# A gated state-space and mixture kernel on one core: input chunks in pairs of 512 columns, and x*D seeded into PSUM before the matmuls

## The chip, the cores and the metric

The kernel runs on one core of one Trainium2 chip. The metric is the device time of one execution in microseconds (us), the median over several runs. The time before was 252.28 us (251.54 to 252.75, three runs). The kernel's own *span* in a profile is 1.7 to 1.9 us shorter than the time in the same run; profile positions below are counted from the span's start. PE is TensorE (matmuls), PEld its weight loads, DVE is VectorE, ACT is ScalarE, POOL is GpSimd, SP is SyncE. PSUM is the memory that matmuls write and accumulate into. "PEclk" is the share of the full TensorE clock that was granted.

## The reference, cut to what matters

```python
x = A_x                                             # (1, 2048, 1024) bf16
g = sigmoid((x * gate_w).sum(-1, keepdims=True))    # one gate per token

# A: a state-space model with a diagonal recurrence over 2048 tokens
Bu = einsum("bld,pd->blp", x, B_bar)                # complex
h_t = Lam_bar * h_(t-1) + Bu_t
a = 2 * einsum("blp,dp->bld", h, C).real + x * Dskip

# B: a small expert for the 8 tokens with the largest r = x @ w_r
idx = argsort(-r)[:8];  xs = x[idx]
y = (silu(xs @ w_gate) * (xs @ w_up)) @ w_down      # 1024 -> 3584 -> 1024
b = x  with  sigmoid(r[idx]) * y  added at idx

out = g * a + (1 - g) * b
```

## The kernel before

Tokens are handled in eight chunks of 256, or sixteen row blocks of 128. *S1* computes V = B x for a chunk (1024 matmuls of 256 columns in all). VectorE turns V by sine and cosine tables, runs the recurrence as a scan, and turns back to H. *S2* computes C H for a row block (512 matmuls). ScalarE empties PSUM: V out of S1, and the gated output out of S2.

```python
def s1u(k, cp, c, pl):            # 8 matmuls, 256 columns wide
    ...
    for dc in range(KD):
        nc.tensor.matmul(vps[:, pl, c, :], lhsT=BT[pl][:, dc, ct * P:(ct + 1) * P],
                         rhs=xT[k][:, dc, :], start=(dc == 0), stop=(dc == KD - 1))

def s1e(k, cp):                   # ScalarE empties the bank pair
    nc.scalar.copy(out=V[k][:, :, 2 * cp:2 * cp + 2, :], in_=vp.pop((k, cp))[:])
...
def scale_x(b):                   # ScalarE: the factor g*D + (1-g) of a row block, f32
    es[b] = gpool.tile([P, D], F32, name="e32", tag="e32")
    nc.scalar.activation(out=es[b][:], in_=Dbc[:], func=ACT.Identity,
                         scale=gcol[:, b:b + 1], bias=omgcol[:, b:b + 1])

def mul_e(b):                     # VectorE: x * factor, an f32 operand; stored as the first part of the output
    xt = xts[b]
    nc.vector.tensor_tensor(out=xt[:], in0=xt[:], in1=es.pop(b)[:], op=ALU.mult)
    if b < NTT - 2:
        nc.gpsimd.dma_start(out2d[b * P:(b + 1) * P, :], xt[:])
...
def s2(b, dh):                    # 16 matmuls, 512 columns wide; the output is added in memory by fin(b)
    zps = ps_s2.tile([P, 512], F32, name="zps", tag="zps")
    for ct in range(NCT):
        for pl in range(2):
            nc.tensor.matmul(zps[:], lhsT=H[k][...], rhs=CT[pl][:, ct, dsl],
                             start=(ct == 0 and pl == 0), stop=(ct == NCT - 1 and pl == 1))
    nc.scalar.activation(out=ots[b][:, dsl], in_=zps[:], func=ACT.Copy, scale=gcol[:, b:b + 1])

def fin(b):
    nc.gpsimd.dma_start(out2d[b * P:(b + 1) * P, :], ots.pop(b)[:], accum_op=ALU.add)
```

The expert's weights (22 MB) stream through buffers that the chunks of x have left. `load_w` loads the next piece as soon as a buffer is free, and a buffer is free when the matmuls on its old piece are done. So between two bursts of expert matmuls lies a *refill window*, in which the pieces for the next burst have to arrive.

```python
def load_w():
    while nload[0] < NW and free_w:
        ...
        nc.sync.dma_start(...)           # wgu: 448 KB, wd: 512 KB a piece
def moe_item(i):
    w, pool, tag = wq.pop(i)
    ...                                  # matmuls on this piece
    free_w.append((pool, tag))
    load_w()
...
gu_pos = [(4, 3)] * 4 + ...              # where in the order each gate/up piece is used
d_pos = [(7, 4)] * 7 + [(8, 4)] * 7      # the down projection: two bursts of seven pieces
at((8, 4.15), fin_a)                     # then the update is finished and scattered
at((8, 4.17), lambda: (fin_b(), scatter_upd()))
```

A position (n, i) is a place in the order of TensorE's work: stage n, after its unit i.

## Time and profile before

| | before |
|---|---|
| time, median (range) | 252.28 us (251.54 to 252.75) |
| span of the profiled run | 251.0 us |
| PE busy | 243.4 us, 97% |
| DVE busy | 232.9 us, 93% |
| S1 matmuls | 1024 of 256 columns, 114.3 us |
| last product of VectorE that S2 needs | ends at 241.6 us |
| wait of PE for expert weights | none |

The page of the kernel before: busy time by engine; PE, granted clock and DMA in 40 slices of the span (a 9 is 90% or more); the chain of waits by engine and by line; and the costliest group of matmuls (busy us, mean ns of one, idle before).

```profile
PE 243.4 (97%) x1970; PEld 164.1 (65%) x1986; DVE 232.9 (93%) x230; ACT 101.3 (40%) x143; POOL 41.6 (17%) x58
...
PE   7799999999999999999999999999999999999994
...
PEclk9999999999999999999999999999999999999999
...
PE 77%; SPq 18%; DMA 2%; issue 1%; DVE 0%
...
L253 PE MATMUL vps<-xT,BT 128*128 128x256 bf16 x1024 | 114.3, 273 | 2.0 <-DMA BT<-in_A_B_re_dram 0.9
```

TensorE is busy from the first slice to the last, at full clock, and the chain of waits is mostly its own work. The mean of 273 ns is the latency of one matmul; what counts is the distance between two of them, read from a stretch in the timeline: 64 matmuls of 256 columns take 7.15 us there (112 ns each at the edges of a stretch, 109 in the middle).

### The profile page before, as it was taken

How to read it: one execution, taken by the hardware profiler on the slowest of the kernel's cores; microseconds unless marked ns; L12 is line 12 of the kernel's file. 1: busy time of each engine (PE TensorE's matmuls, PEld its weight loads, DVE VectorE, ACT ScalarE, POOL GpSimd, SP SyncE). 2: the span in 40 equal slices, each digit the busy share in tenths (PEclk: the TensorE clock that was granted, in tenths of full speed). 3: DMA queues.
4: the chain of work that ended last, by engine and by line, in shares of the span. 5: the costliest groups of instructions: out<-in, count | busy, mean ns of one | idle time of the engine just before them, and what ended most of it. 6: DMA issues, size and time to landing. Idle time of an engine off the chain costs nothing.

```text
span 251.0 us, 4661 instructions
## 1 busy us (share of the span) xinstructions
PE 243.4 (97%) x1970; PEld 164.1 (65%) x1986; DVE 232.9 (93%) x230; ACT 101.3 (40%) x143; POOL 41.6 (17%) x58
## 2 busy tenths in 40 slices
PE   7799999999999999999999999999999999999994
PEld 5588889884668547874477744886448864454453
DVE  1899999999999499999999999999999999999993
ACT  3679992525213321634221371221722335264411
POOL 4020000000000057301400140013100500141520
PEclk9999999999999999999999999999999999999999
DMA  7999999999920202809795588759998739957082
GB/s 167 212 184 221 190 218 246 232 216 278 278 93 3 73 0 86 170 9 346 149 357 181 206 224 280 248 215 335 269 309 273 187 68 292 301 134 198 3 167 84
DMA packets 63492, 48.31 MB, mean 192 GB/s; under 512 B 49504, under 2 KB 51168, under 8 KB 63472
## 3 DMA queue, kind: packets, MB, share of 16 engines
q1 hardware_dynamic: 59056, 37.23, 57.5%
q0 software_dynamic: 4224, 10.53, 17.4%
q8 instruction: 15, 0.25, 0.4%
q10 hardware_dynamic: 192, 0.27, 0.3%
q14 instruction: 5, 0.04, 0.1%
HBM read 27.55 MB, written 8.40 MB: 143 GB/s over the span
## 4 chain that ended last, share of the span: by engine, by line
PE 77%; SPq 18%; DMA 2%; issue 1%; DVE 0%
PE zps L716 41%; PE vps L253 28%; SPq L89 8%; SPq L98 8%; PE zl L730 3%; PE pgu L635 3%; DMA xT<-in_A_x_dram 2%; SPq L85 2%; PE y L647 1%; PE zc L468 1%; SPq L77 0%; DVE ot L735 0%; PE aT_ps L662 0%; PE xselT_ps L561 0%; PE zs_ps L577 0%
## 5 line engine op out<-in xcount | busy, mean ns | idle before, releaser
L253 PE MATMUL vps<-xT,BT 128*128 128x256 bf16 x1024 | 114.3, 273 | 2.0 <-DMA BT<-in_A_B_re_dram 0.9
L253 PEld LDWEIGHTS <-BT 128*128 128x128 bf16 x1024 | 99.4, 98 | 16.4 <-issue 2.3
L716 PE MATMUL zps<-CT,H 128*128 128x512 bf16 x465 | 104.0, 379 | 1.0 <-issue 0.3
L716 PEld LDWEIGHTS <-H 128*128 128x128 bf16 x480 | 46.2, 98 | 55.8 <-issue 1.9
L288 DVE TENSOR_TENSOR_SCAN U<-d,U 128x2048 bf16<-128x2048 f32 (+1 forms) x20 | 61.7, 3127 | 0.4
L258 ACT CAST V<-vps 128x1024 bf16<-128x1024 f32 x32 | 32.2, 1008 | 60.3 <-PE vps L253 60.3
L719 ACT ACTIVATE ot<-zps,gcol 128x512 bf16<-128x512 f32 x30 | 20.6, 687 | 67.9 <-PE zps L716 67.9
L693 POOL DMA_DIRECT2D out_dram<-xt x14 | 7.8, 559 | 93.2 <-DVE xt L691 92.6
L687 ACT ACTIVATE e<-Dbc,omgcol,gcol 128x1024 f32<-128x1024 bf16 x16 | 18.9, 1233 | 0.0
L691 DVE TENSOR_TENSOR xt<-xt,e 128x1024 bf16<-128x1024 bf16 x16 | 18.8, 1218 | 0.0
L278 DVE TENSOR_TENSOR V<-V,nTi 128x4096 bf16<-128x4096 bf16 (+1 forms) x10 | 16.5, 1652 | 0.5
L277 DVE TENSOR_TENSOR U<-V,T2tab 128x4096 bf16<-128x4096 bf16 (+1 forms) x10 | 16.5, 1646 | 0.5
L279 DVE TENSOR_TENSOR U<-U,V 128x4096 bf16<-128x4096 bf16 (+1 forms) x10 | 16.5, 1652 | 0.3
L554 POOL DMA_INDIRECT xsel<-in_A_x_dram,idx_c x1 | 6.4, 6383 | 61.6 <-ACT ot L719 61.6
L313 DVE TENSOR_TENSOR U<-U,S2tab 128x4096 bf16<-128x4096 bf16 (+1 forms) x8 | 16.2, 2025 | 0.3
L315 DVE TENSOR_TENSOR H<-H,U 128x4096 bf16<-128x4096 bf16 (+1 forms) x8 | 16.2, 2025 | 0.3
L311 DVE TENSOR_TENSOR H<-U,Ctab 128x4096 bf16<-128x4096 bf16 (+1 forms) x8 | 16.1, 2018 | 0.0
L740 POOL DMA_DIRECT2D out_dram<-ot x14 | 14.3, 1044 | 2.0 <-ACT ot L719 2.0
L682 POOL DMA_DIRECT2D xt<-in_A_x_dram x12 | 8.2, 680 | 13.6 <-DMA out_dram<-xt 13.6
L346 DVE TENSOR_TENSOR_SCAN U<-D,U 128x1024 bf16<-128x1024 f32 x4 | 8.9, 2278 | 0.0
L635 PE MATMUL pgu<-wgu,xsel 128*32 128x448 bf16 x128 | 7.4, 355 | 0.0
L730 PE MATMUL zl<-CT,H 128*128 128x256 bf16 (+1 forms) x47 | 7.1, 306 | 0.1
(145 smaller groups left out, 128.4 us busy)
## 6 DMA issues: line engine op xcount, KB each, us to landing
wgu<-in_B_w_gate_dram SPq DMA_DIRECT2D x16, 448.0 KB, 5.8
wgu<-in_B_w_up_dram SPq DMA_DIRECT2D x16, 448.0 KB, 5.9
wd<-in_B_w_down_dram SPq DMA_DIRECT2D x12, 512.0 KB, 6.4
out_dram<-xt POOLq DMA_DIRECT2D x14, 256.0 KB, 2.9
out_dram<-ot POOLq DMA_DIRECT2D x14, 256.0 KB, 5.7
xt<-in_A_x_dram POOLq DMA_DIRECT2D x12, 256.0 KB, 4.9
xt<-in_A_x_dram SPq DMA_DIRECT2D x4, 256.0 KB, 4.8
wd<-in_B_w_down_dram SPq DMA_DIRECT2D x4, 256.0 KB, 7.3
```

The source lines that it names most:

```text
L89: nc.sync.dma_start_transpose(BT[pl][:, :, c0 * P:c1 * P], Bsrc[pl][c0 * P:c1 * P, :])
L98: nc.sync.dma_start_transpose(CT[pl][:, :, d0_:d0_ + 512], Csrc[pl][d0_:d0_ + 512, :])
L253: nc.tensor.matmul(vps[:, pl, c, :], lhsT=BT[pl][:, dc, ct * P:(ct + 1) * P], rhs=xT[k][:, dc, :], start=(dc == 0), stop=(dc == KD - 1))
L258: nc.scalar.copy(out=V[k][:, :, 2 * cp:2 * cp + 2, :], in_=vp.pop((k, cp))[:])
L277: nc.vector.tensor_tensor(out=u, in0=v, in1=T2tab[:, :, c0:c1, :], op=ALU.mult)
L278: nc.vector.tensor_tensor(out=v, in0=v, in1=bc(nTi, c0, c1), op=ALU.mult)
L279: nc.vector.tensor_tensor(out=u, in0=u, in1=V[k][:, ::-1, c0:c1, :], op=ALU.add)
L288: nc.vector.tensor_tensor_scan(out=fl, data0=d0[:, c0:c1, :].rearrange("p c t -> p (c t)"), data1=fl, initial=0.0, op0=ALU.mult, op1=ALU.add)
L687: nc.scalar.activation(out=es[b][:], in_=Dbc[:], func=ACT.Identity, scale=gcol[:, b:b + 1], bias=omgcol[:, b:b + 1])
L691: nc.vector.tensor_tensor(out=xt[:], in0=xt[:], in1=es.pop(b)[:], op=ALU.mult)
L716: nc.tensor.matmul(zps[:], lhsT=H[k][:, pl, ct, tl * P:(tl + 1) * P], rhs=CT[pl][:, ct, dsl], start=(ct == 0 and pl == 0), stop=(ct == NCT ...
L719: nc.scalar.activation(out=ots[b][:, dsl], in_=zps[:], func=ACT.Copy, scale=gcol[:, b:b + 1])
```

## The change

Its intent is to give TensorE fewer and wider matmuls, and to take work from VectorE. Chunks of x lie in pairs, so that most of S1 runs with 512 columns. The gates of all tokens come from 32 wide matmuls instead of 128 narrow ones. From row block 4 on, VectorE computes x*D in bf16, ScalarE copies it into the PSUM bank of S2, and S2's matmuls add onto it; ScalarE scales x by 1 - g for the first part of the output. All of S1 now runs earlier, and the order at the end is S2 of chunks 4 to 7 back to back. The expert's weights come in slots of two pieces, in four big buffers.

```diff
-            nc.tensor.matmul(vps[:, pl, c, :], lhsT=BT[pl][...], rhs=xT[k][:, dc, :], ...)
+        o = vp[m, ct][:, pl, k0:k1, :].rearrange("p k t -> p (k t)")
+            nc.tensor.matmul(o, lhsT=BT[pl][...], rhs=X[m][:, dc, k0 * LC:k1 * LC], ...)
...
-    def gate_cols(k0, k1):
-                    nc.tensor.matmul(zc[:, j, :], lhsT=xT[k][:, dc, tl * P:(tl + 1) * P], rhs=rg[:, dc, :], ...)
+    def gate_rows():
+                nc.tensor.matmul(zr[32 * m:32 * m + 32, :], lhsT=rg[:, dc, :], rhs=X[m][:, dc, :], ...)
...
+    def skip_d(k):
+        for b in (2 * k, 2 * k + 1):
+            xd[b] = xdpool.tile([P, D], BF16, name="xd", tag="xd")
+            nc.vector.tensor_tensor(out=xd[b][:], in0=xts[b][:], in1=Dbc[:], op=ALU.mult)
+    def skip_x(*bs):
+        for b in bs:
+            nc.scalar.activation(out=xt[:], in_=xt[:], func=ACT.Copy, scale=omgcol[:, b:b + 1])
+            if b < NTT - 2:
+                nc.scalar.dma_start(out2d[b * P:(b + 1) * P, :], xt[:])
+    def preset(b, dh):
+            z = pool.tile([P, w], F32, name="zps", tag=tag)
+            nc.scalar.copy(out=z[:], in_=xd[b][:, d_:d_ + w])
...
-                nc.tensor.matmul(zps[:], ..., start=(ct == 0 and pl == 0), ...)
+                nc.tensor.matmul(zps[:], ..., start=(fresh and ct == 0 and pl == 0), ..., skip_group_check=not fresh)
...
-    d_pos = [(7, 4)] * 7 + [(8, 4)] * 7
+    pos = ... + [(7, 0.9)] * 2 + [(8, 1.9)] * 4 + [(9, 0.9)] * 3        # slots of two pieces
+        at(pos[s], lambda s=s: moe_slot(s))
-    at((8, 4.15), fin_a)
+    at((9, 0.92), fin_a)
```

The down projection now has a burst of four slots (eight pieces) and one of three (six pieces), and its second burst stands three S2 units behind the first, where before it stood four behind.

## The prediction

> **What bounds it now.** TensorE. The busy table gives PE 243.4 of 251.0 us (97%) at full clock; the chain of waits is almost all matmuls (L716 41%, L253 28%) after the transposing loads of the start. VectorE is nearly co-critical: 232.9 us; its timeline has one gap over 1 us between 12 and 246 us (3.1 us at 84 us), and its last scan product ends at 241.6 us, just before the final matmuls (240.6 to 247.7) need it. ScalarE has 40%.
>
> **Removed.**
> - S1 goes from 1024 matmuls of 256 columns to 480 of 512 plus 64 of 256. In the windows view an undisturbed S1 stretch takes 13.95 us for 128, 109 ns each; S2's 512-column ones take about 213. Only about 2.5 ns per removed matmul go: about 1.5 us, perhaps 3 us with the early ones (110 to 112 ns). The Trainium skill ("TensorE: Matmul & The Clock Gate", section "Wait — 56ns, not 53.3ns?") gives 2.5 ns fixed per warm matmul; the trace agrees.
> - Gate columns: 128 small matmuls (3.5 us) become 32 wide ones in four column groups plus four transposes, an estimate of 2.3 us from the 57 ns of the grouped MoE matmuls: 1.2 us less.
> - VectorE: twelve of sixteen f32-operand skip products (1.22 us) become bf16 products (0.68 us, as the bf16 add of that shape): 6.5 us less. Six gate operations go to ACT: 1 us.
>
> **Added.** ScalarE: 24 preset copies into PSUM and 12 row scalings replace twelve 1.23 us scalings; S1 drains are twice as many, half as wide; about 10 us more, hidden: presets are issued before the previous drain. The risk is correctness: the skill's "PSUM — Partial Sum Buffer", section "The four PSUM rules", says engine writes do not set the bits that make a matmul accumulate; the bank must have been written by matmuls before, and it has.
>
> **Moved.** All S1 now runs earlier, S2 of blocks 4 to 7 back to back at the end. Walking the new order by hand with trace durations:
> - VectorE waits about 1.4 us at the start, since V0 is complete only after six paired column tiles, and still ends its last product near 236 to 237 us, 4 to 5 us earlier than before.
> - PE's gate pass needs the last x chunk near 61 us, about 1 us after PE gets there.
> - The token gather now ends near 104 us (index near 95, plus 8 to 9 us as in the trace), while PE wants it for its transposes near 101.5: a PE wait of about 2 to 3 us that before did not exist (before: landed 98.6, used 107.3).
> - MoE weights come in pairs into four big slots; at the late bursts the refill windows (12 to 14 us for about 3 MB) leave little margin: 0 to 2 us.
>
> **On the critical path.** PE saves about 4 us, plus about 1 us of early waits, and gives back about 3 us in new waits. VectorE's 4 us become slack. Predicted: 249.4 us, range 246.0 to 252.8. Faster by over 2%: 0.17; within 2%: 0.77; slower: 0.06.
>
> **What would show it.** S1 at about 213 ns per 512-column matmul; PE busy near 239 us; skip products at 0.68 us and VectorE near 226 us; PE idle before the gate pass (about 1 us) and before the gathered-token transposes (2 to 3 us); no PE wait on presets; VectorE waiting in the final blocks or finishing over 2 us before the last matmuls.
>
> **What would make it wrong.** A gather faster than assumed (then near 247); PE waiting for weights longer; ScalarE late with drains or presets, because its own output-DMA issues wait in its queue; VectorE still gating the last blocks.

## More of the kernel before

The end of TensorE's timeline before: start us, length us, group, and in brackets any wait before it. The lines with `y<-wd,aT` are the two bursts of the down projection.

```profile
206.11 1.71 PE L647 MATMUL y<-wd,aT 128*32 128x256 bf16 x56
207.98 13.76 PE L716 MATMUL zps<-CT,H 128*128 128x512 bf16 x62 [0.16 <-issue]
221.67 1.71 PE L647 MATMUL y<-wd,aT 128*32 128x256 bf16 x56
223.31 17.44 PE L716 MATMUL zps<-CT,H 128*128 128x512 bf16 x78
240.59 7.11 PE L730 MATMUL zl<-CT,H 128*128 128x512 bf16 x47
```

The second burst starts at 221.67 with no bracket behind it, so it did not wait. The refill window is 221.67 - 206.11 = 15.6 us. How much of it the transfers needed is in the windows view of the same stretch (window, busy us of each engine, granted clock, share of the 16 DMA engines that was busy, GB/s):

```profile
216.00:218.00 2.00, 2.00 (x11) 0.93 (x10) 2.00 (x3) 0.00 (x0) 0.56 (x1) 1.00 1.04 320
218.00:220.00 2.00, 1.95 (x10) 0.88 (x10) 2.00 (x2) 0.69 (x1) 0.54 (x1) 1.00 1.07 402
220.00:222.00 2.00, 2.00 (x21) 0.91 (x22) 2.00 (x2) 0.22 (x1) 0.00 (x0) 1.00 0.39 156
```

The DMA engines are full until 220 us and fall quiet before 222. The last load of these weights was issued at 210.6 us and took 11.6 us to land, so it landed at 222.2, 16.1 us after the first burst began; the matmuls on its piece, the seventh, started at 223.0.

## The result, and the profile after

| | before | after |
|---|---|---|
| time, median (range), 4 runs each | 252.51 us (251.54 to 252.93) | 255.94 us (255.70 to 256.63) |
| ratio | | 1.0146, 95% interval 1.0108 to 1.0183 |
| span of the profiled run | 251.0 us | 254.8 us |
| PE busy | 243.4 us | 245.1 us |
| DVE busy | 232.9 us | 227.1 us |
| wait of PE for expert weights | 0 | 3.8 us |
| mean granted clock | 0.999 (profiled run) | 0.984 to 0.993 |

A ratio is the mean time of one kernel's fast runs over that of the other's from the same rounds, so it is not quite the ratio of the medians. The changed kernel is correct, and 1.5% slower.

The page of the kernel after, the same parts:

```profile
PE 245.1 (96%) x1414; PEld 115.7 (45%) x1414; DVE 227.1 (89%) x231; ACT 117.5 (46%) x203; POOL 33.5 (13%) x50
...
PE   7899999999999999999999999999999999589995
...
PEclk9999999999999999999999999999999999959999
...
PE 85%; DMA 9%; SPq 4%; issue 0%; DVE 0%
...
L771 PE MATMUL zps<-CT,H 128*128 128x512 bf16 x480 | 108.1, 386 | 0.0
L266 PE MATMUL vps<-X,BT 128*128 128x512 bf16 x480 | 105.3, 379 | 0.2 <-DMA BT<-in_A_B_im_dram 0.2
L282 PE MATMUL vps<-X,BT 128*128 128x256 bf16 x64 | 7.3, 273 | 1.2 <-DMA BT<-in_A_B_re_dram 0.8
```

Most of it went as intended: S1 costs 105.3 + 7.3 = 112.6 us instead of 114.3, VectorE lost 5.8 us of work. But slice 35 of PE has a 5, and the granted clock has a 5 one slice later. The end of TensorE's timeline after:

```profile
206.48 1.93 PE L672 MATMUL y<-wd,aT 128*32 128x256 bf16 x64
208.34 10.53 PE L771 MATMUL zps<-CT,H 128*128 128x512 bf16 x48
218.81 1.06 PE L672 MATMUL y<-wd,aT 128*32 128x256 bf16 x32
221.61 0.40 PE L672 MATMUL y<-wd,aT 128*32 128x256 bf16 x8 [1.74 <-DMA wd<-in_B_w_down_dram]
224.11 0.62 PE L672 MATMUL y<-wd,aT 128*32 128x256 bf16 x8 [2.09 <-DMA wd<-in_B_w_down_dram]
224.66 20.07 PE L771 MATMUL zps<-CT,H 128*128 128x512 bf16 x80
244.56 7.11 PE L787 MATMUL zps<-CT,H 128*128 128x512 bf16 x48
```

The second burst now starts 218.81 - 206.48 = 12.3 us after the first. The last two pieces are not there: TensorE waits 1.74 and 2.09 us. And then 80 matmuls take 20.07 us. At the pace of the stretch between the bursts (48 in 10.53 us, with the latency of the last counted in) they would take about 17.4. The windows view of the same stretch, same columns, says why:

```profile
218.00:220.00 2.00, 1.87 (x37) 1.05 (x35) 1.97 (x4) 0.69 (x1) 0.00 (x0) 1.00 1.06 401
220.00:222.00 2.00, 0.39 (x8) 0.20 (x8) 1.97 (x3) 0.00 (x0) 0.00 (x0) 1.00 1.11 291
222.00:224.00 2.00, 0.01 (x3) 0.00 (x0) 1.97 (x3) 0.00 (x0) 0.00 (x0) 0.80 0.13 27
224.00:226.00 2.00, 1.89 (x12) 0.65 (x12) 1.97 (x3) 1.20 (x4) 0.00 (x0) 0.50 0.00 0
...
228.00:230.00 2.00, 2.00 (x6) 0.76 (x5) 2.00 (x2) 0.00 (x0) 1.31 (x1) 0.50 0.00 0
230.00:232.00 2.00, 2.00 (x10) 0.88 (x9) 2.00 (x2) 1.05 (x2) 2.00 (x1) 1.00 0.00 0
```

Up to 222 us the DMA engines are full (1.06, 1.11): there was more to carry than the window had time for. That is not the whole of it. The last load landed only at 224.06 us, 17.6 us after the first burst began, and in the last 1.5 us before that the DMA share was 0.07 or less, about one engine of the 16. Why that tail is there, no run shows. Then the clock falls to a half, from 223.2 to 230.0 us: six matmuls in 2 us instead of eleven. The page calls that "busy". In the chain of waits of the kernel after (start us, length us, what), the two steps before the last pieces' matmuls are loads of weights, where the kernel before had matmuls:

```profile
207.15 4.63 DMA wd<-in_B_w_down_dram
211.79 12.27 DMA wd<-in_B_w_down_dram
```

The second of them, the last load, was issued only when the first had landed (207.15 + 4.63 = 211.78); SyncE's queue stood still for 1.0 us before it, which in the kernel before it did not.

The sum over TensorE's end closes. Its last group ends 3.97 us later than before (251.67 against 247.70). The waits are 3.83 us, and the half clock costs about 2.7 us in the 80 matmuls and 0.2 in the last eight of the burst. So without the two, TensorE would have ended 2.8 us *earlier* than before.

### The profile page after: what moved, and what is told of

Read it like the earlier page. It is cut to its first block, busy times and chain, and to the rows that moved or that the text cites. A ratio compares the mean times of both kernels' runs of the same rounds, so it can differ in the third digit from the quotient of the medians.

```text
span 254.8 us, 3609 instructions
## 1 busy us (share of the span) xinstructions
PE 245.1 (96%) x1414; PEld 115.7 (45%) x1414; DVE 227.1 (89%) x231; ACT 117.5 (46%) x203; POOL 33.5 (13%) x50
## 4 chain that ended last, share of the span: by engine, by line
PE 85%; DMA 9%; SPq 4%; issue 0%; DVE 0%
PE vps L266 40%; PE zps L771 38%; DMA wd<-in_B_w_down_dram 7%; SPq L80 3%; PE zps L787 3%; PE pgu L660 3%; DMA BT<-in_A_B_im_dram 2%; SPq L93 1%; PE zr L487 1%; PE y L672 0%; SPq L77 0%; DVE ot L792 0%; PE aT_ps L685 0%; PE xselT_ps L579 0%; PE zs_ps L595 0%
## 5 line engine op out<-in xcount | busy, mean ns | idle before, releaser
L266 PE MATMUL vps<-X,BT 128*128 128x512 bf16 x480 | 105.3, 379 | 0.2 <-DMA BT<-in_A_B_im_dram 0.2
L266 PEld LDWEIGHTS <-BT 128*128 128x128 bf16 x480 | 46.3, 98 | 57.0 <-issue 0.8
L313 DVE TENSOR_TENSOR_SCAN U<-d,U 128x2048 bf16<-128x2048 f32 (+2 forms) x22 | 62.0, 2861 | 1.0 <-DVE U L304 0.5
L273 ACT CAST V<-vps 128x512 bf16<-128x512 f32 x60 | 32.2, 588 | 56.7 <-PE vps L266 56.7
L302 DVE TENSOR_TENSOR U<-V,T2tab 128x4096 bf16<-128x4096 bf16 (+2 forms) x11 | 16.6, 1509 | 0.8 <-ACT V L273 0.5
L303 DVE TENSOR_TENSOR V<-V,nTi 128x4096 bf16<-128x4096 bf16 (+2 forms) x11 | 16.7, 1516 | 0.5
L304 DVE TENSOR_TENSOR U<-U,V 128x4096 bf16<-128x4096 bf16 (+2 forms) x11 | 16.7, 1516 | 0.4
L338 DVE TENSOR_TENSOR U<-U,S2tab 128x4096 bf16<-128x4096 bf16 x7 | 16.0, 2292 | 0.2
L340 DVE TENSOR_TENSOR H<-H,U 128x4096 bf16<-128x4096 bf16 x7 | 16.0, 2292 | 0.2
L336 DVE TENSOR_TENSOR H<-U,Ctab 128x4096 bf16<-128x4096 bf16 x7 | 16.0, 2285 | 0.0
```

What stands on the lines that cost most here:

```text
L266: nc.tensor.matmul(o, lhsT=BT[pl][:, dc, ct * P:(ct + 1) * P], rhs=X[m][:, dc, k0 * LC:k1 * LC], start=(dc == 0), stop=(dc == KD - 1))
L273: nc.scalar.copy(out=V[k][:, :, ct, :], in_=vp[m, ct][:, :, kk, :])
L302: nc.vector.tensor_tensor(out=u, in0=v, in1=T2tab[:, :, c0:c1, :], op=ALU.mult)
L303: nc.vector.tensor_tensor(out=v, in0=v, in1=bc(nTi, c0, c1), op=ALU.mult)
L304: nc.vector.tensor_tensor(out=u, in0=u, in1=V[k][:, ::-1, c0:c1, :], op=ALU.add)
L313: nc.vector.tensor_tensor_scan(out=fl, data0=d0[:, c0:c1, :].rearrange("p c t -> p (c t)"), data1=fl, initial=0.0, op0=ALU.mult, op1=ALU.add)
```

## The experiments

My theory: the whole loss is the refill window of the last burst, 3.3 us shorter than before, through a wait and through the clock that the wait cost. Rivals: the wait is only a symptom and something else binds right behind it (VectorE, the scatter of the update); or the loss is in the change's own operations (wide matmuls, presets in ScalarE).

All twelve experiments gave correct results. They ran in three jobs, each with its own runs of the kernel before (medians 252.59, 252.12, 251.97 us):

| run | base, edit | median us | ratio to before (95%) |
|---|---|---|---|
| y_later | after, last burst one unit later | 250.46 | 0.9917 (0.9881 to 0.9953) |
| filler | after, dummy matmuls in the wait | 253.95 | 1.0061 (1.0024 to 1.0098) |
| stores_later | after, four stores out of the window | 262.78 | 1.0406 (1.0357 to 1.0456) |
| before_y_earlier | before, last burst one unit earlier | 258.52 | 1.0254 (1.0196 to 1.0312) |
| y_later_again | = y_later | 250.69 | 0.9941 (0.9903 to 0.9978) |
| s1_256 | y_later, S1 256 wide | 253.36 | 1.0014 (0.9955 to 1.0072) |
| no_preset | y_later, old skip path | 257.76 | 1.0226 (1.0188 to 1.0264) |
| y_first_earlier | after, first burst one unit earlier | 251.14 | 0.9949 (0.9898 to 0.9999) |
| both_y | both bursts moved | 250.35 | 0.9937 (0.9901 to 0.9973) |
| y_later_third | = y_later | 251.57 | 0.9981 (0.9950 to 1.0011) |
| no_preset2 | no_preset, rearranged | 256.28 | 1.0161 (1.0128 to 1.0194) |
| s1_256_again | = s1_256 | 253.22 | 1.0034 (0.9991 to 1.0078) |

The same kernel y_later came out between 0.9917 and 0.9981 in three jobs. Ratios of different jobs are therefore not compared to better than about 0.6%. The medians are over all runs of a label; three labels have one run of the slow state each, and without it their medians are 253.11 (s1_256), 253.03 (s1_256_again) and 250.97 us (y_first_earlier). Three times lie just outside what was expected: y_later, filler and before_y_earlier, by 0.2 to 0.5 us.

### y_later: a longer window

```diff
-    pos = ... + [(8, 1.9)] * 4 + [(9, 0.9)] * 3
+    pos = ... + [(8, 1.9)] * 4 + [(9, 1.9)] * 3
-    at((9, 0.92), fin_a)
+    at((9, 1.92), fin_a)
-    at((9, 0.95), lambda: (fin_b(), scatter_upd(), last_scan(1)))
+    at((9, 1.95), lambda: (fin_b(), scatter_upd(), last_scan(1)))
```

> Changed kernel, but the last three pairs of down weights are used half a row block later (after the second S2 half of block 6's first rows instead of after the first). Theory A (the refill of the weight slots takes about 14 us and PE arrives after 12.3 us; PE waits 3.8 us, then runs about 6 us at half clock and loses another 3 us): PE wait for weights under 0.7 us, mean granted clock 0.999, time 249.5 us (248.8 to 250.3). Rival B (the end is set by VectorE, the scatter or ScalarE, and the wait only hides it): 253 us or more, with a new wait at the end.

Measured: 250.46 us, 0.9917. TensorE's timeline of y_later:

```profile
206.61 1.93 PE L672 MATMUL y<-wd,aT 128*32 128x256 bf16 x64
...
222.39 1.28 PE L672 MATMUL y<-wd,aT 128*32 128x256 bf16 x40
224.15 0.40 PE L672 MATMUL y<-wd,aT 128*32 128x256 bf16 x8 [0.49 <-DMA wd<-in_B_w_down_dram]
224.48 13.99 PE L771 MATMUL zps<-CT,H 128*128 128x512 bf16 x62
238.31 7.11 PE L787 MATMUL zps<-CT,H 128*128 128x512 bf16 x48
```

With a window of 15.8 us the wait is 0.49 us, the clock stays full (0.999 in the profiled run), and the end comes 2.3 us before that of the kernel before. Nothing was left behind the wait that would have held TensorE up. Moving three slots by one unit of 3.5 us is worth 1.0146 - 0.9917 = 2.3%, 5.8 us. This refutes both rivals as the main cause. (The two ratios are of different rounds; with the weakest of the three ratios of this kernel, 0.9981, it is 1.7%. The span difference of the two profiled runs is 254.8 - 248.6 = 6.2 us.)

### filler: the clock without the wait's end

Eighteen matmuls whose result nobody reads, in the very place of the two waits. They shorten nothing; they only keep TensorE running.

```diff
         for i in range(2):
+            if s == NS - 1:
+                if i == 0:
+                    M["fill"] = ps_m.tile([P, 512], F32, name="fill", tag="m")
+                for _ in range((8, 10)[i]):
+                    nc.tensor.matmul(M["fill"][:], lhsT=CT[0][:, 0, 0:P], rhs=CT[0][:, 0, 0:512], start=True, stop=True)
             moe_item(2 * s + i, wq[s][0][:, i])
```

> Changed kernel with 18 matmuls of 512 columns on data that nobody reads, put where PE waits for the last pair of down weights (8 before its first, 10 before its second item, about 3.9 us). Theory A: the weights are as late as before, but PE does not idle, so the clock stays at 1.0 and about 3 us of the slowdown go: 252.9 us (252.0 to 253.7). Rival C (the clock drop costs nothing, or is not caused by the idle time): unchanged, 255.5 to 256.5.

Measured: 253.95 us, 1.0061. TensorE's timeline of filler:

```profile
220.01 1.90 PE L652 MATMUL fill<-CT 128*128 128x512 bf16 x7
221.84 0.40 PE L677 MATMUL y<-wd,aT 128*32 128x256 bf16 x8
222.18 2.33 PE L652 MATMUL fill<-CT 128*128 128x512 bf16 x10
224.44 0.40 PE L677 MATMUL y<-wd,aT 128*32 128x256 bf16 x8
224.77 17.44 PE L776 MATMUL zps<-CT,H 128*128 128x512 bf16 x78
```

The burst ends at the same place as in the kernel after (224.8), and the stretch behind it takes 17.44 us instead of 20.07. The clock was 0.999 or 1.000 in all six runs. So the loss splits: what the clock cost is 1.0146 - 1.0061 = 0.85%, 2.1 us; what the wait itself cost is 1.0061 - 0.9917 = 1.44%, 3.6 us, close to the 3.8 us that the wait view of the kernel after shows. The first difference is between ratios of different jobs, so it is good to some 0.6% only; in the traces the same part is 2.6 us in the long stretch and 0.2 in front of it. One thing stays open: of the four runs of the kernel after, two had a mean clock of 0.984 or 0.985 and two of 0.992 or 0.993, about half as much time at half clock, but their spans do not follow it (254.0 and 254.8 against 253.9 and 254.3 us).

### stores_later: less to carry in the window

The stores of row blocks 12 and 13 and the accumulating stores of row blocks 10 and 11, 256 KB each, are issued after the weights have landed, which takes 1.05 MB out of the window.

```diff
-            if b < NTT - 2:
+            if b < 12:
                 nc.scalar.dma_start(out2d[b * P:(b + 1) * P, :], xt[:])
+    def late_store(b):
+        nc.scalar.dma_start(out2d[b * P:(b + 1) * P, :], xts[b][:])
-    at((8, 2.5), lambda: fin(10))
-    at((8, 3.95), lambda: fin(11))
+    at((9, 1.0), lambda: (late_store(12), late_store(13), fin(10)))
+    at((9, 1.01), lambda: fin(11))
```

> Changed kernel, but four transfers of 256 KB each (the skip stores of rows 12 and 13 and the accumulating stores of rows 10 and 11) are issued only after the last down weights are used; the weights stay where they are. Theory A with shared DMA bandwidth: 3.1 instead of 4.15 MB must pass in the refill window, so the last weights land about 3.4 us earlier, near 219 to 221 us; PE waits 0 to 1.5 us and keeps its clock: 249.5 to 251.5 us. Rival D (the weights are late because of their issue order or their latency, not the bandwidth): wait and time unchanged, 255 to 256.5.

Measured: 262.78 us, and a flawed experiment as a timing: the late stores stood in ScalarE's order behind something that came later still, and TensorE then waited 8.3 us for the next preset. But the waits in front of that are usable. TensorE's timeline of stores_later:

```profile
221.97 0.40 PE L672 MATMUL y<-wd,aT 128*32 128x256 bf16 x8 [1.69 <-DMA wd<-in_B_w_down_dram]
223.08 0.40 PE L672 MATMUL y<-wd,aT 128*32 128x256 bf16 x8 [0.70 <-DMA wd<-in_B_w_down_dram]
...
238.81 11.95 PE L774 MATMUL zps<-CT,H 128*128 128x512 bf16 x47 [8.32 <-ACT zps L748]
```

The wait for weights fell from 3.8 to 2.4 us. From 206 to 224 us the kernel after carried 4.21 MB, of which 3.15 were on the weights' queue, 0.52 on the queue of the accumulating stores and 0.52 on that of ScalarE's stores; here it was 3.16 MB. So what else moves in the window can be part of its price, 1.4 us at most. That is less than was expected: at the pace of the kernel after (4.16 MB in 208 to 222 us, 297 GB/s) 1.05 MB would be 3.5 us. And even this 1.4 us need not be the stores' alone: the last load of weights was issued 4.2 us after the first burst began here, and 5.3 us in the kernel after, where it was held until the first had landed. The run does not tell the two apart. With the weights alone in the window, the last of them still landed 16.1 us after the first burst began, and again the DMA engines were almost idle before that (0.07 or less from 221 us on). The rival that the issue or the latency of the loads has a part in the wait is not excluded. The last bracket shows the other side of the preset: it stands in ScalarE's program order, so one late item there stops TensorE.

### before_y_earlier: the same fault put into the kernel before

```diff
-    d_pos = [(7, 4)] * 7 + [(8, 4)] * 7
+    d_pos = [(7, 4)] * 7 + [(8, 3)] * 7
-    at((8, 4.15), fin_a)
+    at((8, 3.15), fin_a)
```

> Kernel before, with its second seven down-weight items used half a row block (3.4 us) earlier, so that its refill window is 12.2 us as in the changed kernel. Theory A: the last weights land near 221 us as before, PE now reaches them near 218.3 and waits about 2.5 us, then perhaps some us at half clock: 255 to 258 us. Rival E (the changed kernel is slow for a reason of its own, such as the copies into PSUM): within 1 us of the kernel before.

Measured: 258.52 us, 1.0254. TensorE's timeline of before_y_earlier:

```profile
206.09 1.71 PE L647 MATMUL y<-wd,aT 128*32 128x256 bf16 x56
...
220.60 0.40 PE L647 MATMUL y<-wd,aT 128*32 128x256 bf16 x8 [0.93 <-DMA wd<-in_B_w_down_dram]
222.49 0.62 PE L647 MATMUL y<-wd,aT 128*32 128x256 bf16 x8 [1.49 <-DMA wd<-in_B_w_down_dram]
...
244.88 7.11 PE L730 MATMUL zl<-CT,H 128*128 128x512 bf16 x47
```

The window is 12.1 us; TensorE waited 0.93 and 1.49 us for weights, and the clock was 0.50 in the window 222 to 224 us and 0.67 in the next. TensorE ended 4.3 us later than in the kernel before (251.99 against 247.70): 2.4 of that are the waits. So the fault is the place of the burst: it does to the kernel before what it does to the kernel after (a wait of 2.4 us there, 3.8 here), with none of the wide matmuls, presets or big slots present. Here the four runs do show the clock's part: spans of 255.3 and 255.5 us at a mean clock of 0.993, and 258.0 and 258.1 at 0.984 and 0.985.

### y_later_again and y_later_third: how well does it repeat

> The same kernel as y_later, run again so that the next two can be compared with it on one chip: 250.4 us, ratio to before about 0.992.

> The same kernel as y_later, again, as base for the others of this job on this chip: 250.3 to 250.8, ratio 0.991 to 0.995.

Measured: 250.69 us (0.9941) and 251.57 us (0.9981). The last misses what was expected. Its clock was full in all six runs, and the profiled run, its fastest, waited about as long for the weights as the others (0.7 us; 0.5 and 0.7). The difference between jobs is not explained.

### y_first_earlier: the window longer at its other end

```diff
-    pos = ... + [(8, 1.9)] * 4 + [(9, 0.9)] * 3
+    pos = ... + [(8, 0.9)] * 4 + [(9, 0.9)] * 3
-    at((8, 0.8), silu_t)
+    at((7, 3.96), silu_t)
```

> Changed kernel with the last three weight pairs where the change has them, but the first four used one S2 half earlier (and the transposes of the activations before them one half earlier too). Theory A (it is the length of the refill window, from first use to second, that counts): the window is 15.7 us again, the wait under 1 us and the clock 1.0: 249.5 to 251 us. Rival (the last weights are late because of something at that time, whatever came before): wait of 3 us or more, 254 us or more.

Measured: 250.97 us over its four fast runs, 0.9949, all four at full clock. The profiled run is the fifth, slow (254.75 us); it waited 2.51 us, with the DMA at only some 250 GB/s from 208 to 216 us. No trace shows the wait of a fast run. By the times, moving the other end of the window helps as well.

### both_y: both ends

The edits of y_later and y_first_earlier together.

> The changed kernel with the first four of the last seven down-projection slots one tile earlier AND the last three one tile later, so that the refill window is about 17.5 us (y_later had about 14 to 15.7, and still waited 0.5 to 0.7 us). My theory (the weights' refill window is all that was lost): no TensorE wait for wd at all, granted clock 1.0 in the last stretch, time 249.5 to 250.5, ratio about 0.988 to 0.993. Rival (something else in the tail, such as the scatter or VectorE, bounds the end once the wait is short): no gain or a loss against y_later_third, though the wait is gone.

Measured: 250.35 us, 0.9937; y_later_third on the same chip and in the same rounds had 251.57, 0.9981. TensorE's timeline of both_y:

```profile
204.41 1.93 PE L672 MATMUL y<-wd,aT 128*32 128x256 bf16 x64
206.27 17.44 PE L771 MATMUL zps<-CT,H 128*128 128x512 bf16 x78
223.64 1.49 PE L672 MATMUL y<-wd,aT 128*32 128x256 bf16 x48
225.07 13.99 PE L771 MATMUL zps<-CT,H 128*128 128x512 bf16 x62
```

The window is 19.2 us, and no wait for weights is left. The DMA engines fell quiet between 222 and 224 us, 18 us after the first pieces were released, so they used the time that they were given. An earlier first burst is not passed on in full, though: it began 2.1 us earlier than in the kernel after (204.41 against 206.48), and the last weights landed 1.0 us earlier (223.03 against 224.06). The profiled run has a mean clock of 0.993 all the same; its half clock lies at 7.8 to 11.2 us, at the start of the kernel, as in the profiled run of y_later_again. This is the version that beats both kernels: 0.6% faster than before. Its advantage over y_later_third, 0.44%, is no larger than what y_later varied between jobs.

### s1_256 and s1_256_again: what the wide matmuls are worth

y_later, with each 512-column matmul of S1 as two of 256.

```diff
-        for dc in range(KD):
-            nc.tensor.matmul(o, lhsT=BT[pl][...], rhs=X[m][:, dc, k0 * LC:k1 * LC], ...)
+        for k in reversed(range(k0, k1)):
+            for dc in range(KD):
+                nc.tensor.matmul(vp[m, ct][:, pl, k, :], lhsT=BT[pl][...], rhs=X[m][:, dc, k * LC:(k + 1) * LC], ...)
```

> y_later with S1 in matmuls of 256 columns again (960 in place of 480; everything else as in y_later). My reading (a matmul of 512 columns takes 216 ns and two of 256 take 218, so the wide ones save a fixed 2 ns or so each): 1.0 to 1.2 us slower than y_later, 251.5 us. Rival (wide matmuls matter more, for example through half as many weight loads): 3 us or more slower.

> The same kernel as s1_256 (y_later with S1's matmuls 256 columns wide again), whose six times scattered over 4 us. By the pitch of the matmuls alone (two of 109.0 against one of 216 to 217 ns, 480 pairs) it should be slower than y_later_third by 0.5 to 1 us: 250.9 to 251.8, ratio 0.995 to 0.999. Rival (256-wide matmuls also cost something else, as 253.4 hinted): 253 or more again, ratio 1.000 or more.

Measured: 253.36 us and 253.22 us; against y_later of the same job, 0.7% and 0.5% slower (1.0014 / 0.9941 and 1.0034 / 0.9981), 1.8 and 1.3 us. From the intervals of the four ratios these are uncertain by about 0.7% and 0.5%, so hardly clear of noise. In the groups, S1's 960 narrow matmuls take 106.3 us in both runs, where the 480 wide ones take 105.3 in the kernel after (all 480 recorded there). So 1.0 us is the matmuls themselves; in a stretch, 64 narrow ones take 7.15 us and 32 wide ones 7.07. The other 0.3 to 0.8 us and the scatter of the times (250.27 to 253.78 us in the fast runs of the first) stay open; both profiled runs show a slower start of S1 (8.2 and 8.8 us for its first 64 matmuls, which are the same in all these kernels, against 7.3 in y_later), but so does that of y_later_again (8.6); the first has a wait of 0.6 us for x before the gates. The measured sizes miss what I had expected the second time, and neither theory of that expectation is settled.

### no_preset and no_preset2: what the presets are worth

y_later, with the skip path of the kernel before (f32 factor from ScalarE, f32 product on VectorE) for all row blocks, and no seed in PSUM.

```diff
     def skip_d(k):
         for b in (2 * k, 2 * k + 1):
-            xd[b] = xdpool.tile([P, D], BF16, name="xd", tag="xd")
-            nc.vector.tensor_tensor(out=xd[b][:], in0=xts[b][:], in1=Dbc[:], op=ALU.mult)
+            for i, e in enumerate(es.pop(b)):
+                nc.vector.tensor_tensor(out=xt[:, i * 512:(i + 1) * 512], in0=xt[:, i * 512:(i + 1) * 512], in1=e[:], op=ALU.mult)
     def preset(b, dh):
-        if b < 2 * KX:
-            return
+        return
 # rows_e(3) to rows_e(8) added to the order; in no_preset2 rows_e(4), rows_e(5) and skip_d(3) stand later
```

> y_later with the skip path of the kernel before for all row blocks: no copies into PSUM, no bf16 products, no row scalings; VectorE multiplies by the f32 factor (2.49 us per block in place of 1.29). My reading (VectorE gains 7 us from the change, of which it now has 4 to 6 us as slack): VectorE busy 234 us, its last product near 243 us, PE or the last adds wait for it, 2 to 3 us slower than y_later: 252.5 us (251.3 to 254). Rival (the slack is large enough, so the second half of the change brings nothing): within 0.6 us of y_later.

> As no_preset (y_later with the f32 skip path of the kernel before for all blocks, no presets), but ScalarE's factor rows of blocks 6 and 7 come after VectorE has freed the buffers, and VectorE's products for them stand before the scan of chunk 4. Then ScalarE does not stop TensorE in mid-kernel. VectorE's products cost 6.5 us more, its last product for the scanned states ends near 242 to 243 us and TensorE wants the second half near 240. If the presets and bf16 products are worth only VectorE slack, the time is that of y_later_third plus 0 to 2 us of TensorE wait at the last block (ratio 0.993 to 1.002). Rival (VectorE as co-critical as TensorE, so its 6.5 us came through in full): 255 or more, with TensorE waiting on VectorE in the last blocks.

Measured: 257.76 us (1.0226) and 256.28 us (1.0161). Both are confounded. The f32 factors sit in a buffer of two row blocks. ScalarE had to wait for VectorE to give it back, and TensorE then waited for ScalarE in the middle of the kernel. no_preset2 took away one such place of two. TensorE's timeline of no_preset2:

```profile
112.77 0.37 PE L660 MATMUL pgu<-wgu,xsel 128*32 128x448 bf16 x4
117.13 1.31 PE L660 MATMUL pgu<-wgu,xsel 128*32 128x448 bf16 x12 [3.98 <-ACT zs_b L597]
```

That wait of 3.98 us again halved the clock, from 115 to 122 us. The wait and the half clock behind it cover the loss against y_later (256.28 - 251.57 = 4.7 us in the same job), and no wait for VectorE is seen in the last blocks. So these runs do not say what VectorE's 6.5 us are worth on their own. They say that in this order the old path stops TensorE where the new one does not. VectorE's last product came at 243.4 us and the last group of matmuls at 244.4; had TensorE been on time (238.3 in y_later), it would have had to wait for VectorE. That is an inference, not a measurement.

## Why the prediction was wrong, point by point

**The step that failed** is the last of the moved items: "at the late bursts the refill windows (12 to 14 us for about 3 MB) leave little margin: 0 to 2 us". The place and the mechanism are right. The size is wrong twice. First, the wait was 3.8 us. The estimate set about 3 MB against the length of the window; what counts is when the last piece lands and when it is wanted. In the trace before, that was 16.1 us after the burst began, with a margin of 0.8 us. The new order took 3.3 us off the window, so about 2.5 us of wait come from this alone (an estimate; before_y_earlier, with 3.5 us taken off, waited 2.4). The rest, about 1.4 us, is what stores_later took away: it had 1.05 MB of stores less in the window, which the estimate had left out, and issued the last load 1.1 us earlier after the start of the burst. How it divides between these two stays open. Second, nothing in the prediction says that a wait of this length costs clock: another 2.1 us by the filler run, 2.9 us in the profiled run. A term of 0 to 2 us became about 6.

**The sum of the savings** was a little too large. It says TensorE saves "about 4 us, plus about 1 us of early waits". The groups give 1.7 us for S1 and 1.2 for the gates (3.5 us before; 1.9 + 0.4 after), 2.9 in all. The early waits hardly changed (2.0 us before S1's matmuls, 1.4 after). The kernel without a wait for weights, both_y, is 0.6% faster than before, 1.6 us.

**The waits that did not come.** The prediction had 1 us before the gate pass and 2 to 3 us before the gathered tokens. There was neither: S1 runs into the gate pass at 60.54 us without a gap, and the gather landed 3.7 us after its issue at 96.4 us, where the trace before had 7.8 (GpSimd's own instruction took 2.4 us there and 6.4 before); TensorE took the tokens at 101.3. So two errors worked against each other: a wait of 3 to 4 us that was not there against one of 6 that was. Also, the terms as written add up to a gain of 2 us (250.3 us), and the time that was given, 249.4, is 0.9 below that.

**What was right.**
- S1's wide matmuls: 43.34 us for 200 in the kernel after, 216 to 217 ns each (the latency of the last is counted in) against two of 109; predicted about 213. Small, as predicted. The Trainium skill ("TensorE: Matmul & The Clock Gate", section "Wait — 56ns, not 53.3ns?") gives 2.5 ns of fixed cost per warm matmul on top of the columns at 2.4 GHz; the estimates from it are 512/2.4 + 2.5 = 215.8 and 256/2.4 + 2.5 = 109.2 ns, and the trace agrees within about 1 ns.
- The skip products: 0.684 us mean (predicted 0.68). VectorE 227.1 us busy (about 226). Its last product ends at 237.0 us (236 to 237).
- ScalarE has 16 us more work (predicted 10) and no preset held TensorE in the kernel after. The gate pass cost 2.3 us, as predicted.
- The seeds in PSUM were correct in every run. The skill's "PSUM — Partial Sum Buffer", section "The four PSUM rules", calls zero the only seed that is safe either way, because writes of ScalarE and VectorE do not change the bit that makes a matmul add; here the banks had been fully written by matmuls before, and no run shows a wrong sum.
- "PE busy near 239 us" was wrong: 245.1. About 2.9 us of that is time at half clock, which counts as busy; y_later, at full clock, has 241.3.

## What to carry to other kernels

When the order of work changes, list each place where a buffer is refilled and read from the trace when its last transfer lands and when it is wanted; a window that shrinks by more than that margin becomes a wait. Count *all* that the DMA engines carry in it, not the new transfer alone. A change that saves 3 us on the bound engine is easily outweighed by one window that shrinks by 3 us: here the repair was to move three items by one unit. And read the granted clock next to every wait of TensorE: a wait of 2 to 4 us can cost as much again behind it, in time that the profile calls busy; matmuls without use, put into the wait, show how much.

## What the Trainium skill lacked or had wrong

- "TensorE: Matmul & The Clock Gate", section "What's actually happening", has the clock fall after an idle window of about 3.4 us, free-running. The traces agree in size: half clock in mid-kernel lasted 6.83 us (the kernel after, no_preset2) or 3.41 us (before_y_earlier, no_preset), two such windows or one. But shorter waits were enough: 1.74 + 2.09 us with 0.4 us of work between them gave 6.83 us of half clock, and 0.93 + 1.49 us (before_y_earlier) 3.41 us; 1.69 + 0.70 us (stores_later) and a single 2.04 us (no_preset) gave none. Section "Why this matters for your kernels" of the page asks for no gaps over about 3 us; by these runs, two gaps that add up to 2.4 us can already cost clock, and need not.
- No page that I read has the experiment that takes the clock's cost apart from the wait's: eighteen matmuls without use, put into the wait. By it, the clock was 2.1 us of 5.8.
- No page that I read has the time from issue to landing of a small gather: the same eight rows took 7.8 us in the kernel before and 3.7 in the kernel after.
